# Moving the weight tiles of a float32r FFN within SBUF: one offset modulo 512 bytes for each f pair

## The chip, the cores and the metric

One Trainium2 chip, one of its cores. The metric is device microseconds of one execution, as the median of several executions. The kernel before takes 973.74 us (three runs, 971.68 to 973.83).

## The reference

Eight batches of eight heads, 576 positions, head size 64, in float32. Each head gets two attentions, whose results are added: one over q, k and v averaged over groups of four positions (144 by 144, each result repeated four times), and one over the full positions with a band mask of |i - j| < 4. The result, transposed to 4608 tokens by 512, goes through a feed-forward network (FFN):

```python
h = x @ w_in                      # 4608x512 @ 512x2048
g = s * np.maximum(h, 0.0)**2 + b
out = g @ w_out                   # 4608x2048 @ 2048x512
```

## The kernel before

The FFN fills most of the time. Its tokens are cut into 18 blocks t of 256, its 2048 hidden columns into 8 pairs p of two 128-column tiles (an f pair). Every float32 operand is split into two float32r parts, a high one and a rest, and a product is the sum of three matmuls (high by high, high by rest, rest by high).

`gemm1(t, p)` (L539) takes 24 matmuls of 256 columns, lines 544 to 546: the stationary operand, loaded ahead of each matmul, is a 128x128 piece of `wi[p]`, the moving operand a 128x256 piece of the block's `xh` or `xl`. ACT and DVE then make the parts of g (`gh`, `gl`, or one tile `gb` that holds both). `gemm2(t, p)` (L574) takes 12 matmuls of 512 columns, lines 589 to 591: here the stationary operand is a 128x128 piece of g, and the moving operand is a 128x512 piece of `wo[p]`. So the weights are stationary in gemm1 and moving in gemm2. Over the 18 blocks that is 3456 matmuls of gemm1 and 1728 of gemm2. A list `order` (L641 to L644) gives the steps: blocks 0 and 1 alternate over p, then block 2, then block by block; gemm2 runs two or three steps behind gemm1. From block 3 on, the pairs 2 and 5 use `gb`, which lies in the memory of tag `xl2` (L548).

The attention (`first_unit`, `down_unit`, `local_unit`) is woven between those steps by a generator. `split_x(t)` (L517) makes `xh` and `xl`: in tiles of those names, two of each, but for block 2 in the tiles of tags `os` and `xl2`. The weights are split by `split_parts(p)` (L239) out of staged loads (`load_w`, L196).

Where a tile lies in SBUF follows from the code alone. There are three pools, `cst`, then `one`, then `two`, each right behind the other. A pool gives every tag its place in the order in which the tags are first asked for; a tag takes the size of its largest tile, rounded up to 32 bytes of each partition, times the pool's buffers. The first tile lies at byte 1152. `make_room` (L88) asks for wi5 and wo5, then wi4, wo4, wi2 and `os`, then wi3, wo3, wo2 and `xl2`, as scratch for the first attention units before the weights move in; `load_w(0)` asks for wi6 and wo6, the first attention unit for its small tiles, `split_w(0)` for wi0 and wo0, `load_w(2)` for wi7 and wo7, and `split_w(1)` for wi1 and wo1. Each of these weight tiles takes 8192 bytes, so none changes the offset modulo 512 of what follows; the smaller tiles do. This gives, in bytes modulo 512:

```
tile                                    before
wi, wo of pairs 2, 3, 4, 5, 6              352
wi, wo of pairs 0, 1, 7                    480
xh, xl (blocks other than 2), gh, gl       288
os, xl2 (x's parts of block 2; gb)         352
```

Inside its tile, every piece that a matmul reads begins at a multiple of 512 bytes. The matmuls' tiles of 128 columns take 512 bytes of each partition, those of 256 take 1024, those of 512 take 2048. All SBUF that the kernel may use is taken.

The small tiles that the change touches are `mask` (L131), read by two DVE casts (L148, L149) at the start, `ptm` (L318), written by ACT (L319) and read by two matmuls (L328), and `ups` (L409), written by ACT from those matmuls' result (L410) and read by DVE (L423).

Of the kernel before, what the change touches and what calls it, by code (L numbers as in the profile page):

```python
# [10 lines left out]
F32 = mybir.dt.float32  # L11
# [7 lines left out]
P = 128  # L19
# [3 lines left out]
SD = S // FAC  # L23
# [31 lines left out]

W_MAX = (1.875 - 2.0 ** -23) * 2.0 ** (31 - 127)

OB = {0: (0, 1), 1: (2, 3), 2: (6, 7)}


@with_exitstack
def attention_ffn_kernel(ctx, tc, qk, vw_in, vr_in, vdm, qkn, vn, w_in, w_out, s_in, b_in, out):
# [3 lines left out]
    cst = ctx.enter_context(tc.tile_pool(name="cst", bufs=1))  # L66
    one = ctx.enter_context(tc.tile_pool(name="one", bufs=1))
    two = ctx.enter_context(tc.tile_pool(name="two", bufs=2))
    ps = ctx.enter_context(tc.tile_pool(name="ps", bufs=1, space=PS))

    def bank(i, shape, name):
        return ps.tile(shape, F32, tag=f"k{i}", name=name)
# [10 lines left out]
    def flat(tag, n, pool=one):  # L83
        return pool.tile([P, n], F32, tag=tag, name="flat")

    room = {}

    def make_room(i):  # L88
        sc, dg = flat(f"wi{6 - i}", 2048), flat(f"wo{6 - i}", 2048)
        if i == 1:  # L90
            big = flat("x", HP * S, two)
            lp = {"vw": take(big, 0, [P, NG, P]), "vd": take(big, 768, [KM, FAC, P])}
            pl, at = big, 1280
        else:
            big = flat("wi2" if i == 2 else "wo2", 2048)
            pl, at = flat("os" if i == 2 else "xl2", 1024), 512
            lp = {"qk": take(big, 0, [P, 2, SP]), "vw": take(big, 2 * SP, [P, NG, P]),
                  "vd": take(pl, 0, [KM, FAC, P])}
        lp["vr"] = take(sc, 1792, [P, FAC, D])
        return {"sc": sc, "dg": dg, "load": lp, "pl": take(pl, at, [P, 2 * NG, 32]),  # L100
                "sm": take(pl, at + 384, [P, 2, 2 * NG])}
# [26 lines left out]

    mask = cst.tile([P, 3, 32], F32, name="mask")  # L131
    nc.gpsimd.memset(mask, 0.0)

    def keep(ap, pattern, base, cm):
# [61 lines left out]
    def load_w(p):  # L196

        parts = (("i", src_i[:, :, 512 * p : 512 * p + 512]), ("o", src_o[:, 2 * p : 2 * p + 2]))
        for op, src in parts:
            st = one.tile([P, 1024, 2], I32, tag=f"w{op}{STAGE[p]}", name="wst")  # L200
            nc.sync.dma_start(st.rearrange("p (k f) t -> p k (f t)", k=src.shape[1]), src)
            wst[(p, op)] = st
# [34 lines left out]
            split_parts(p)  # L237

    def split_parts(p):  # L239
        wi[p] = one.tile([P, 2, NK, 256], F32R, tag=f"wi{p}", name="wi")  # L240
        wo[p] = one.tile([P, 2, 2, DM], F32R, tag=f"wo{p}", name="wo")
        for op, w in (("i", wi[p]), ("o", wo[p])):
            fl = w.rearrange("p s k f -> p s (k f)")
            if p < len(STAGE):
                st = wst.pop((p, op))
                for j in range(0, 1024, CHUNK[p]):
                    js = slice(j, j + CHUNK[p])
                    convert(st[:, js], fl[:, 0, js], fl[:, 1, js], op, p)
            else:
                for i in range(4):  # L250
                    cs = slice(256 * i, 256 * i + 256)
                    convert(load_quarter(p, op, i), fl[:, 0, cs], fl[:, 1, cs], op, p)
# [80 lines left out]
    def first_unit(b, hp, banks):  # L333

        alt = hp if b == 0 else 0
        at = 0
        if alt:
            sc = room[hp]["sc"]
        spots = {}

        def tmp(shape, name):
            nonlocal at
            if not alt:
                return one.tile(shape, F32, tag=name, name=name)

            if name in ("ups", "ptr"):
                spots[name] = spots["qd" if name == "ups" else "kd"]
            else:
                spots[name] = at
                at += math.prod(shape[1:])  # L350
            return take(sc, spots[name], shape)

        x = new_x(b)
        tqk, vw, _, _ = ld[(b, hp)]
        qt, kt = tqk[:, 0], tqk[:, 1]
        dg = diag[alt]
        bd = dg[0]
        dn = down(b, hp, banks, tmp, dg)
        next(dn)
        yield  # L360
        next(dn)
        yield

        own = room[hp] if b == 0 and hp else None
        pl = own["pl"] if own else two.tile([P, 2 * NG, 32], F32, tag="pl", name="pl")
        sm = own["sm"] if own else two.tile([P, 2, 2 * NG], F32, tag="sm", name="sm")
        lmx, lsm = sm[:, 0], sm[:, 1]
        for h in range(2):  # L370
            sl = banks([P, NG, 32], "sl")
            nc.tensor.matmul(sl, idb, maskb, start=True, stop=False)
            hs = slice(64 * h, 64 * h + 64)
            for g in range(NG):
                for w in range(4):
                    c0 = TW * (4 * g + w)
                    nc.tensor.matmul(
                        sl[32 * w : 32 * w + 32, g, :],
                        qt[hs, c0 : c0 + 32], kt[hs, c0 : c0 + 32],
                        start=False, stop=g == NG - 1, tile_position=(64 * h, 32 * w))  # L380
            hg = slice(h * NG, h * NG + NG)
            nc.vector.tensor_reduce(lmx[:, hg], sl, AX.X, ALU.max)
            nc.vector.tensor_tensor(
                pl[:, hg], sl, lmx[:, hg].unsqueeze(2).to_broadcast([P, NG, 32]), ALU.subtract)
            yield
        nc.scalar.activation(pl, pl, AF.Exp, scale=SCALE)
        nc.vector.tensor_reduce(lsm, pl, AX.X, ALU.add)
        nc.vector.tensor_scalar(lsm, lsm, 1e-9, None, ALU.add)
        nc.vector.reciprocal(lsm, lsm)
        (nc.vector if b else nc.gpsimd).tensor_tensor(  # L390
            pl, pl, lsm.unsqueeze(2).to_broadcast([P, 2 * NG, 32]), ALU.mult)
        yield
        next(dn)
        yield
        next(dn)
        if own:
            pt = take(sc, spots["vt"], [P, 2 * NG, 32])
        else:
            pt = two.tile([P, 2 * NG, 32], F32, tag="pl", name="pt")
        nc.vector.transpose(pt, pl)  # L400
        for w in range(4):
            ws = slice(32 * w, 32 * w + 32)
            nc.scalar.copy(bd[ws, :, ws], pt[ws])
        yield
        try:
            next(dn)
        except StopIteration as e:
            up = e.value
        ups = tmp([P, SD], "ups")  # L409
        nc.scalar.copy(ups, up)  # L410
        yield
        for f in range(2):
            n = S // 2 // FAC
            ol = banks([P, S // 2], "ol")
            for gg in range(NG // 2):
                g = f * (NG // 2) + gg
                for h in range(2):
                    hs = slice(64 * h, 64 * h + 64)
                    pw = bd[:, h * NG + g, :].rearrange("p (w c) -> p w c", w=4)
                    nc.tensor.matmul(  # L420
                        ol[hs, 96 * gg : 96 * gg + 96], vw[:, g, hs], pw[:, :, 0:TW],
                        start=True, stop=True)
            nc.vector.tensor_tensor(  # L423
                x[:, hp, f * (S // 2) : (f + 1) * (S // 2)].rearrange("p (s j) -> p s j", j=FAC),
                ol.rearrange("p (s j) -> p s j", j=FAC),
                ups[:, n * f : n * f + n].unsqueeze(2).to_broadcast([P, n, FAC]), ALU.add)
            if f == 1:
                complete.add((b, hp))
            yield
# [87 lines left out]
    def split_x(t):  # L517
        tags = ("os", "xl2") if t == 2 else ("xh", "xl")
        pool = one if t == 2 else two
        xh = pool.tile([P, HP, TB], F32R, tag=tags[0], name="xh")  # L520
        xl = pool.tile([P, HP, TB], F32R, tag=tags[1], name="xl")
        t0 = t * TB
        while t0 < (t + 1) * TB:
            b = t0 // S
            while (b, HP - 1) not in complete:
                next(gen)
            n = min((t + 1) * TB, (b + 1) * S) - t0
            src = xt[b][:, :, t0 - b * S : t0 - b * S + n]
            dst = slice(t0 - t * TB, t0 - t * TB + n)
            nc.scalar.copy(xh[:, :, dst], src)  # L530
            nc.vector.tensor_tensor(
                xl[:, :, dst], src, xh[:, :, dst].bitcast(F32), ALU.subtract)
            t0 += n
        xs[t] = (xh, xl)
# [39 lines left out]
    def gemm2(t, p):  # L574
# [3 lines left out]
        if p == 0:  # L578
            ob = OB.get(t, OB[0])
            oacc[t] = [bank(i, [P, DM], "po") for i in ob]  # L580
# [53 lines left out]
    split_w(0)  # L634
    load_w(1)
    load_w(2)
    split_x(0)
    split_x(1)

# [118 lines left out]
```

## Time and profile before

```
median of three runs        973.74 us
the profiled execution      974.94 us
its span                    973.1 us
matmuls                     7316 records, PE busy 937.4 us (96%)
DVE / ACT / POOL busy       646.8 / 478.8 / 425.0 us
granted TensorE clock       0.982 of full speed over the span
```

The page gives each engine's busy time, the span in forty slices, and the chain of work that ended last. Matmuls are pipelined, so that the duration of one (281 to 284 ns for 256 columns) is longer than the step from one matmul's start to that of the next. For the rate at which TensorE works, the starts in the timeline are what to read: the step is the difference of two starts over the number of matmuls between them.

### The profile page before, as it was taken

The numbers are of one execution on the slowest core, as the hardware profiler recorded it, in microseconds if no ns is written. First come the engines' busy times: TensorE is split into PE (matmuls) and PEld (weight loads), VectorE is DVE, ScalarE is ACT, GpSimd is POOL, SyncE is SP. The second block draws the span as 40 slices with busy tenths as digits, with TensorE's granted clock in tenths as the row PEclk, the third lists the DMA queues.
The fourth block names the chain that finished last, engine by engine and source line by source line (L and its number), as shares of the span: only waits on it lengthen the run. The fifth ranks groups of instructions, "written<-read, shape, count | busy, mean of one in ns | idle before, by whom it ended". The sixth has DMA issues, their size and how long they took to land.

```text
span 973.1 us, 18535 instructions
## 1 busy us (share of the span) xinstructions
PE 937.4 (96%) x7316; PEld 840.0 (86%) x7316; DVE 646.8 (66%) x1175; ACT 478.8 (49%) x1141; POOL 425.0 (44%) x455
## 2 busy tenths in 40 slices
PE   5769999999999999999999999999999999999998
PEld 4558888788999989889989898999899999998997
DVE  5999985864468778878787975876787772211121
ACT  5878775453755454534545344454454444333231
POOL 9422011100167686776767585575776750000000
PEclk9579999999999999999999999999999999999999
DMA  9746422102233232322323232231323100000000
GB/s 314 261 132 204 166 65 73 60 31 86 88 122 112 86 101 85 133 65 72 106 93 102 80 98 80 78 112 58 112 90 111 55 23 1 23 1 22 1 23 22
DMA packets 32103, 86.26 MB, mean 89 GB/s; under 512 B 3344, under 2 KB 7952, under 8 KB 32016
## 3 DMA queue, kind: packets, MB, share of 16 engines
q1 hardware_dynamic: 32016, 85.08, 26.4%
q8 instruction: 57, 0.93, 0.4%
q14 instruction: 30, 0.25, 0.1%
HBM read 75.63 MB, written 9.44 MB: 87 GB/s over the span
## 4 chain that ended last, share of the span: by engine, by line
PE 76%; DVE 7%; POOL 6%; DMA 6%; issue 3%; ACT 2%; DVEq 0%; SPq 0%; POOLq 0%; ACTq 0%
PE ph L544 12%; PE ph L545 12%; PE ph L546 12%; PE po L589 11%; PE po L590 11%; PE po L591 11%; DMA tqk<-in_qk_dram 3%; POOL pr L455 2%; PE sa L297 2%; DMA lqk<-in_qkn_dram 1%; POOL acc L477 1%; DMA wst<-in_moe_w_out_dram 1%; PE up L328 1%; PE ol L420 1%; PE ot L486 1%
## 5 line engine op out<-in xcount | busy, mean ns | idle before, releaser
L544 PE MATMUL ph<-xh,wi 128*128 128x256 f32 x1152 | 327.2, 284 | 5.3 <-DVE gl L557 2.5
L545 PE MATMUL ph<-xl,wi 128*128 128x256 f32 x1152 | 324.0, 281 | 0.0
L546 PE MATMUL ph<-xh,wi 128*128 128x256 f32 x1152 | 323.6, 281 | 0.0
L455 POOL TENSOR_TENSOR pr<-lqk 128x576 f32<-128x576 f32 x140 | 203.0, 1473 | 90.1 <-DMA lqk<-in_qkn_dram 53.9
L544 PEld LDWEIGHTS ph<-xh,wi 128*128 128x128 f32 x1152 | 217.1, 188 | 12.8 <-DVE gl L557 3.4
L545 PEld LDWEIGHTS ph<-xl,wi 128*128 128x128 f32 x1152 | 217.0, 188 | 5.0 <-issue 0.2
L546 PEld LDWEIGHTS ph<-xh,wi 128*128 128x128 f32 x1152 | 217.3, 189 | 0.1
L554 ACT ACTIVATE ph<-ph 128x512 f32<-128x512 f32 x144 | 83.7, 581 | 236.7 <-PE ph L546 236.5
L589 PE MATMUL po<-wo,gh 128*128 128x512 f32 x456 | 183.0, 402 | 0.2 <-ACT gh L556 0.2
L590 PE MATMUL po<-wo,gh 128*128 128x512 f32 x456 | 181.5, 398 | 0.0
L591 PE MATMUL po<-wo,gl 128*128 128x512 f32 x456 | 179.5, 399 | 0.0
L557 DVE TENSOR_TENSOR gl<-ph,gh 128x512 fp32r<-128x512 f32 x114 | 77.9, 683 | 110.9 <-ACT gh L556 110.5
L477 POOL TENSOR_TENSOR acc<-acc,pv 128x576 f32<-128x576 f32 x80 | 114.6, 1433 | 68.0 <-DVE acc L477 33.5
L457 DVE TENSOR_REDUCE st<-pr 128x9 f32<-128x576 f32 x140 | 105.9, 756 | 40.9 <-POOL pr L455 38.8
L287 POOL TENSOR_TENSOR dq<-vq 64x64 f32<-64x64 f32 x58 | 25.6, 441 | 192.4 <-PE up L326 190.2
L556 ACT CAST gh<-ph 128x512 fp32r<-128x512 f32 x114 | 66.8, 586 | 70.6 <-PE po L590 68.5
L591 PEld LDWEIGHTS po<-wo,gl 128*128 128x128 f32 x456 | 85.7, 188 | 17.3 <-issue 0.2
L476 DVE TENSOR_TENSOR pv<-lv,st 128x576 f32<-128x576 f32 x120 | 87.2, 747 | 20.2 <-POOL acc L477 19.6
L589 PEld LDWEIGHTS po<-wo,gh 128*128 128x128 f32 x456 | 85.7, 188 | 15.8 <-ACT gh L556 0.8
L590 PEld LDWEIGHTS po<-wo,gh 128*128 128x128 f32 x456 | 85.8, 188 | 15.6
L555 ACT ACTIVATE ph<-ph 128x512 f32<-128x512 f32 x144 | 83.8, 582 | 3.4
L590 PE MATMUL po<-wo,gb 128*128 128x512 f32 x120 | 48.2, 402 | 0.0
(145 smaller groups left out, 1261.1 us busy)
## 6 DMA issues: line engine op xcount, KB each, us to landing
tqk<-in_qk_dram SPq DMA_DIRECT2D x30, 584.0 KB, 4.0
lqk<-in_qkn_dram SPq DMA_DIRECT2D x20, 768.0 KB, 4.4
lv<-in_vn_dram SPq DMA_DIRECT2D x20, 480.0 KB, 3.5
out_dram<-os SPq DMA_DIRECT2D x17, 512.0 KB, 3.0
wst<-in_moe_w_in_dram SPq DMA_DIRECT2D x7, 1024.0 KB, 5.5
wst<-in_moe_w_out_dram SPq DMA_DIRECT2D x7, 1024.0 KB, 5.3
tvd<-in_vdm_dram SPq DMA_DIRECT2D x29, 160.0 KB, 2.7
tvr<-in_vr_dram SPq DMA_DIRECT2D x29, 128.0 KB, 2.1
```

The lines of the kernel that those rows point to most:

```text
L455: nc.gpsimd.tensor_tensor(pr, lqk[:, 0:CH], lqk[:, CH + o : 2 * CH + o], ALU.mult)
L457: nc.vector.tensor_reduce(ls[:, :, o], pr, AX.X, ALU.add)
L476: nc.vector.tensor_tensor(pv, lv[:, o : o + CH], w, ALU.mult)
L477: (nc.vector if o % 3 == 1 else nc.gpsimd).tensor_tensor(acc[:, :, h], acc[:, :, h], pv, ALU.add)
L544: nc.tensor.matmul(ph[:, j], wi[p][:, 0, k, f], xh[:, k], start=(k == 0), stop=False)
L545: nc.tensor.matmul(ph[:, j], wi[p][:, 0, k, f], xl[:, k], start=False, stop=False)
L546: nc.tensor.matmul(ph[:, j], wi[p][:, 1, k, f], xh[:, k], start=False, stop=(k == NK - 1))
L554: nc.scalar.activation(ph, ph, AF.Relu)
L555: nc.scalar.activation(ph, ph, AF.Square)
L589: nc.tensor.matmul(po[m], gh[:, j, ms], wo[p][:, 0, j], start=first, stop=False)
L590: nc.tensor.matmul(po[m], gh[:, j, ms], wo[p][:, 1, j], start=False, stop=False)
L591: nc.tensor.matmul(po[m], gl[:, j, ms], wo[p][:, 0, j], start=False, stop=last)
```

## The change

A helper `skip(n)` asks for a tile of n bytes in each partition under a tag of its own, which nothing writes or reads. It is called ahead of some of the weight tiles and, in the pool of `xh`, ahead of those. Room for it comes from two small tiles: `mask` goes into the tag `pv`, and the nine units that had `ups` in a tile of its own put it into the tag `ptm`. No instruction is added or taken away.

```diff
+    def skip(n, pool=one):
+        pool.tile([P, n // 4], F32, tag=f"skip{next(skips)}", name="skip")
+    skips = itertools.count()
     def make_room(i):
+        skip(32 if i == 1 else 64)
         sc, dg = flat(f"wi{6 - i}", 2048), flat(f"wo{6 - i}", 2048)
         if i == 1:
...
         else:
+            skip(64)
             big = flat("wi2" if i == 2 else "wo2", 2048)
...
-    mask = cst.tile([P, 3, 32], F32, name="mask")
+    mask = two.tile([P, 3, 32], F32, tag="pv", name="mask")
...
     def load_w(p):
+        if p == 2:
+            skip(64)
...
     def split_parts(p):
+        if p == 1:
+            skip(64)
...
-        ups = tmp([P, SD], "ups")
+        ups = tmp([P, SD], "ups") if alt else one.tile([P, SD], F32, tag="ptm", name="ups")
...
     load_w(2)
+    skip(128, two)
     split_x(0)
```

Worked out in the same way as above, the offsets modulo 512 become:

```
tile                                   before   after
wi5, wo5                                  352       0
wi4, wo4                                  352      64
wi2                                       352     128
wi3, wo3                                  352     192
wo2                                       352     256
wi6, wo6                                  352     256
wi0, wo0                                  480     320
wi7, wo7                                  480     384
wi1, wo1                                  480     448
xh, xl, gh, gl                            288       0
os (xh of block 2)                        352     128
xl2 (xl of block 2; gb)                   352     256
```

Call the distance of a matmul the offset of its weights less that of its x or g, modulo 512. In gemm1 it is, before, 64 for the pairs 2 to 6 and 192 for 0, 1 and 7; in block 2 it is 0 and 128. After, it is 0, 64, 128, 192, 256, 320, 384 and 448 for the pairs 5, 4, 2, 3, 6, 0, 7 and 1. In gemm2 the distances are the same, but for wo2 at 256, and but for pairs 2 and 5 from block 3 on, whose g is `gb`: 0 for both before, 0 and 256 after. Before, every one of these tiles begins 32 bytes past a multiple of 64; after, all of them begin at a multiple of 64.

## Rows read from the trace of the kernel before

**Rows 1.** The page: busy time, granted clock in 40 slices, chain by engine.
```profile
PE 937.4 (96%) x7316; PEld 840.0 (86%) x7316; DVE 646.8 (66%) x1175; ACT 478.8 (49%) x1141; POOL 425.0 (44%) x455
...
PEclk9579999999999999999999999999999999999999
...
PE 76%; DVE 7%; POOL 6%; DMA 6%; issue 3%; ACT 2%; DVEq 0%; SPq 0%; POOLq 0%; ACTq 0%
```

**Rows 2.** Busy time by stage, columns as in the head row.
```profile
core 0: us, PE busy (x) PEld busy (x) DVE busy (x) ACT busy (x) POOL busy (x), PEclk, DMA share, GB/s
0.00:110.00 110.00, 82.87 (x1126) 71.28 (x1127) 97.39 (x198) 80.48 (x202) 43.52 (x87) 0.84 0.68 230
...
300.00:600.00 300.00, 297.23 (x1981) 269.35 (x1980) 237.80 (x413) 137.75 (x342) 212.91 (x196) 1.00 0.30 96
600.00:840.00 240.00, 240.00 (x1601) 218.14 (x1600) 158.20 (x281) 111.90 (x268) 129.16 (x119) 1.00 0.21 67
```

**Rows 3.** What PE waited for, longest in total first: us, times, longest.
```profile
PE sa L297 <- ACT dq L277: 7.3, 1, 7.3
PE ol L420 <- ACT db L403: 4.6, 2, 2.7
...
PE ph L544 <- DVE gl L557: 2.5, 3, 1.2
```

**Rows 4.** PE's timeline, gemm1(17, 2): first and fourth matmul, next stage: start, us.
```profile
930.52 0.28 PE L544 MATMUL ph<-xh,wi 128*128 128x256 f32 x1
...
930.88 0.28 PE L544 MATMUL ph<-xh,wi 128*128 128x256 f32 x1
...
933.25 0.39 PE L589 MATMUL po<-wo,gh 128*128 128x512 f32 x1
```

**Rows 5.** The same view, gemm1(17, 1), first matmul and next stage.
```profile
922.16 0.28 PE L544 MATMUL ph<-xh,wi 128*128 128x256 f32 x1
...
924.99 0.39 PE L589 MATMUL po<-wo,gh 128*128 128x512 f32 x1
```

**Rows 6.** The same view, gemm1(17, 6), first matmul and next stage.
```profile
949.78 0.28 PE L544 MATMUL ph<-xh,wi 128*128 128x256 f32 x1
...
952.61 0.40 PE L589 MATMUL po<-wo,gh 128*128 128x512 f32 x1
```

**Rows 7.** The same view, gemm1(2, 4): two matmuls with 18 steps between.
```profile
193.03 0.28 PE L544 MATMUL ph<-xh,wi 128*128 128x256 f32 x1
...
195.19 0.28 PE L544 MATMUL ph<-xh,wi 128*128 128x256 f32 x1
```

**Rows 8.** The same view, gemm1(2, 1): two matmuls with 18 steps between.
```profile
168.71 0.28 PE L544 MATMUL ph<-xh,wi 128*128 128x256 f32 x1
...
170.85 0.28 PE L544 MATMUL ph<-xh,wi 128*128 128x256 f32 x1
```

**Rows 9.** The same view, gemm2(16, 1): its first matmul, and the next group's.
```profile
897.10 0.39 PE L589 MATMUL po<-wo,gh 128*128 128x512 f32 x1
...
899.88 0.40 PE L589 MATMUL po<-wo,gb 128*128 128x512 f32 x1
```

**Rows 10.** The same view, gemm2(16, 6): two matmuls with six steps between.
```profile
925.68 0.39 PE L589 MATMUL po<-wo,gh 128*128 128x512 f32 x1
...
927.05 0.39 PE L589 MATMUL po<-wo,gh 128*128 128x512 f32 x1
```

**Rows 11.** The same view, gemm2(16, 5) with gb: eleven steps between.
```profile
919.39 0.40 PE L589 MATMUL po<-wo,gb 128*128 128x512 f32 x1
...
921.92 0.40 PE L591 MATMUL po<-wo,gb 128*128 128x512 f32 x1
```

**Rows 12.** Lines 410 and 423: duration min/median/max, first and last start.
```profile
L410 ACT COPY ups<-up x9: 259/279/284, 24.0 to 267.8; 128x144 f32<-128x144 f32 x9
...
L423 DVE TENSOR_TENSOR x<-ol,ups x18: 411/448/458, 31.0 to 269.7; 128x288 f32<-128x288 f32 x18
```

**Rows 13.** Line 149, the last reader of the mask.
```profile
L149 DVE CAST maskb<-mask x1: 403/403/403, 10.9 to 10.9; 128x64 bf16<-128x64 f32 x1
```

## The prediction

> **What bounds the kernel now.** I read the page first: TensorE is busy for 96% of the span, is 76% of the chain that ended last, and from the fifth slice on has its full clock, the 2.4 GHz level [rows 1]. The table by stage then says where it is not the bound: only in the first 110 us, where it is busy for 83 of 110 us at a granted clock of 0.84; from 300 to 600 us it is busy for 297 of 300, from 600 to 840 us for all of it, while VectorE, the next busiest, has 238 of 300 and 158 of 240 [rows 2]. The list of TensorE's waits agrees: its longest items are 7.3 and 4.6 us, both of attention work, and gemm1's wait for g's parts is 2.5 us in all [rows 3]. So behind the first 110 us whatever changes the step from one matmul to the next changes the end by as much, and 3456 matmuls of gemm1 and 1728 of gemm2 turn 1 ns on each into 3.5 and 1.7 us.
>
> The step is therefore the thing to read, from the starts in the timeline. gemm1(17, 2) takes 24 steps in 933.25 - 930.52 = 2.73 us, 113.8 ns each [rows 4]. gemm1(17, 1), the same instructions on other tiles, takes 2.83 us, 117.9 ns each [rows 5]. Nothing waits in either; attention is over by then. I read all 136 groups of gemm1 outside block 2 in this way; each is close to one of those two steps or changes between them once. Of the pairs 0, 1 and 7, at distance 192, 48 of 51 groups are long. Of the pairs 2 to 5, at distance 64, 17 of 68 are long (1, 3, 5 and 8 for pairs 2, 3, 4, 5). But pair 6, also at 64, has 14 of 17 long (2.83 us in the last block) [rows 6]. Block 2, whose x lies elsewhere, has two more: at distance 0 18 steps take 2.16 us, 120.0 ns each [rows 7], at distance 128 2.14 us, 118.9 ns [rows 8].
>
> gemm2 shows the same in weaker form: 231.7 ns at distance 192 (2.78 us over 12) [rows 9], 228.3 at 64 (1.37 over 6) [rows 10], 230.0 at 0 with gb (2.53 over 11) [rows 11].
>
> So where the two operands lie to one another does seem to set the step, but not alone: pair 6 says that the same distance can give either step.
>
> **The change, part by part.** No instruction is added or removed and no queue is reordered by the edit itself, so the sum has two kinds of terms: steps, and waits from shared tiles.
>
> Waits first. `mask` in a buffer of `pv` is last read at 10.9 us by L149 [rows 13]; the next writer of that buffer is the conversion of the first weights, far behind it in program order: 0. If it did wait, it would wait for 0.4 us once. `ups` in `ptm`'s place is written by ACT (L410) from the result of the very matmuls that read `ptm`, so it adds no wait there. The next unit's `ptm` (L319) must now also wait until L423 has read `ups`. L423 takes 0.45 us and there are 18 of it for nine copies [rows 12]; the generator runs a unit to its end before the next one begins, so the reader is one half of an attention unit ahead. Behind L319 on ACT stand the FFN's activations, and TensorE waits for those; with the cover gone it would cost 9 x 0.45 = 4 us at the most. I take 0.
>
> gemm1, blocks other than 2, 17 x 24 = 408 matmuls for each pair:
> Pair 5 goes to distance 0. Block 2 has 120.0 there [rows 7]; now 8 of its 17 groups are long, so it is at (9 x 113.8 + 8 x 117.9)/17 = 115.7. That is +4.3 x 408 = +1.7 us.
> Pair 2 goes to 128: 118.9 [rows 8] against 114.0 now, +4.9 x 408 = +2.0 us.
> Pair 3 goes to 192, where nearly all groups are long: 117.7 against 114.5, +3.2 x 408 = +1.3 us.
> Pair 4 stays at 64: 0.
> Pairs 6, 0, 7 and 1 go to 256, 320, 384 and 448, which no gemm1 of this trace has. The nearest rows bound the step by 113.8 and 120.0 [rows 4, 7]. These pairs are now long in 62 of 68 groups, 117.5. I take the middle of the bounds, 116.9, since four distances that are known (113.8 to 120.0) spread over the whole of them: -0.6 x 1632 = -1.0 us, and from -6.0 to +4.1 us by the bounds.
> Block 2: its `xh` and `xl` now lie at two different offsets, so each pair sees two distances. 192 matmuls, now near 119.7, at the middle: -0.5 us, from -1.1 to 0.
> Together +3.5 us.
>
> gemm2: pairs 0, 1 and 7 leave 192 for distances without a row: bounds 228.3 and 231.7 [rows 9, 10], the middle 230.0, -1.7 x 648 = -1.1 us, from -2.2 to 0. Pair 3 goes from 64 to 192: +3.4 x 216 = +0.7 us. Pairs 5 and 6 go to 256 from 230.0 [rows 11] and 228.3, to the middle again: 0 and +0.4 us, from -0.4 to +1.1 together. Pairs 2 and 4 stay. Sum of gemm2 0.0 us.
>
> Sum +3.5 us: 974.94 becomes 978.4 for the profiled execution. That execution is 1.2 us over the median of its runs, so the median goes from 973.74 to 977.2 us.
>
> Two places where the trace has to be weighed against a rule. The steps at one clock differ by 4 ns between pairs that differ in nothing but place [rows 4, 5]. The Trainium skill, page "TensorE: Matmul & The Clock Gate", section "Step-by-step: what each phase is for", says that the moving operand and the weight load have a read port each, so that loading the next weights takes nothing from the running matmul. By that rule no offset matters and the sum is 0; it is the first rival below, and the trace speaks against it. The second: past its first three matmuls gemm1(17, 2) takes (933.25 - 930.88)/21 = 113 ns a step [rows 4], and no group of the trace is faster, although 256 columns at one a cycle of 2.4 GHz are 106.7 ns. The same page, section "Back-to-back issue gap", gives N/2.4 + 2.5 ns, which is 109.2 here, as the isolated gap; the trace is above it everywhere.
>
> **The rivals.**
> *No effect of the place*: what sets the long or the short step is the order of the work ahead of a group, not the offset; pair 6, long at the distance where others are short, and pair 5, half and half, speak for it; blocks 0 and 1, where pair 6 is short and pair 1 long, and block 2, near 120, speak against it. Order stays, so 973.7 us.
> *The unknown distances are good ones*, the case on the other side (not slower): pairs 6, 0, 7 and 1 lock to the short step, as the pairs at 64 mostly do. Then gemm1 has +5.0 - 6.0 - 1.1 = -2.1 us and gemm2 -2.2 + 0.7 - 0.4 = -1.9 us, together -4.0: 969.7 us. It decides from the point where more than about half of those 68 groups turn short: each is worth 24 x 4.1 ns = 0.1 us. For it: they are long now and have little to lose. Against it: of four known distances only one is short.
> *They are bad ones*: 120.0 in gemm1 for all four, +5.0 + 4.1 = +9.1 us, and +0.7 + 1.1 us in gemm2, +10.9: 984.6 us.
> *The sixteenth goes*: all tiles now begin 32 bytes past a multiple of 64, after at a multiple. The least step, 113 of 106.7 ns, is a sixteenth over a column per cycle. If that sixteenth came from the start inside a 64-byte stretch, 6.7 x 3456 + 13.3 x 1728 = 46 us would go: 928 us. Nothing in the trace has the other alignment for float32r, so it can't be excluded; but an operand that starts half a stretch late would touch one stretch more per matmul, 17 for 16 at 256 columns and 33 for 32 at 512, and gemm2's 228.3 ns [rows 10] are more than a sixteenth over 213.3, not half of that. That speaks against it.
>
> **How the numbers follow.** The sum, 977.2 us, has 0.38; its bounds are the good and the bad case above, and the edge to "no change", 976.7, is close. No effect 0.14, good distances 0.23, bad ones 0.17, the sixteenth 0.08. What a measurement can tell from no change is about 0.3%, 2.9 us. Slower by more than that: a little over half of the first case and all of the bad ones, with some waits, 0.41. Faster by more: most of the good ones and the sixteenth, 0.29. Within it: 0.30. The range of 8 in 10 leaves out the sixteenth and the outer end of the bad and the good ones: 964 to 984 us. The likeliest case's own range is 971 to 983; the 4 us of an uncovered wait would lie within it.
>
> **What would show it right or wrong.** In the timeline of the changed kernel the starts of gemm1's matmuls in the last two blocks: pair 4 stays at 113.8 ns, pair 5 goes to 120, pair 2 to about 119, pair 3 to 117.9; the step of pairs 6, 0, 7 and 1 is the open question, and whether 448 mirrors 64 can be read at once from pair 1. gemm2's pairs 0, 1 and 7 should be at or below 231.7. PE's waits should not grow at L319's readers or at L544. If a pair has the step of before at a new distance, the place does not matter; if any step falls below 113.3 ns, the sixteenth depends on the alignment and the prediction is wrong by far.

## The result, and the profile after

The changed kernel takes 977.98 us (four runs, 977.7 to 978.55) against 973.79 us for the kernel before, of which there are now four runs. The ratio is 1.0045, with a 95% interval of 1.0028 to 1.0061. By the medians it is slower by 4.2 us, where 3.5 were forecast; by the ratio it is 4.4 us. The profiled execution took 978.55 us. Every engine has the same instructions in the same order as before, so only places differ.

First the page of the changed kernel: busy time, clock in 40 slices, chain by engine.

```profile
PE 944.5 (97%) x7316; PEld 846.9 (87%) x7316; DVE 647.3 (66%) x1175; ACT 478.9 (49%) x1141; POOL 423.5 (43%) x455
...
PEclk9969999999999999999999999999999999999999
...
PE 87%; DVE 5%; DMA 2%; POOL 2%; issue 2%; ACT 2%; DVEq 0%; POOLq 0%; SPq 0%; ACTq 0%
```

TensorE is busy 7.1 us longer than in [rows 1] and its weight loads 6.9 us; of the other engines none is busy more than 0.5 us longer. The same table by stage as [rows 2], for the changed kernel:

```profile
0.00:110.00 110.00, 84.50 (x1119) 72.18 (x1120) 96.71 (x196) 80.02 (x200) 42.10 (x87) 0.92 0.68 226
...
300.00:600.00 300.00, 298.89 (x1983) 271.61 (x1982) 238.56 (x413) 139.23 (x349) 214.28 (x198) 1.00 0.30 95
600.00:840.00 240.00, 240.00 (x1600) 218.70 (x1600) 159.07 (x284) 111.24 (x267) 130.31 (x121) 1.00 0.21 68
```

From 300 us on TensorE has its full clock in both kernels and hardly any idle time in either. So the extra time is in what it does, not in what it waits for. Its longest waits after, us in total, times, longest:

```profile
PE sa L311 <- ACT dq L291: 7.3, 1, 7.3
PE ol L434 <- ACT db L417: 4.2, 2, 2.3
...
PE ph L558 <- ACT xh L544: 2.2, 1, 2.2
...
PE ph L558 <- DVE gl L571: 1.2, 2, 1.0
```

They answer to [rows 3] (lines are 14 further on), item by item. The only new item of the whole list is one of 0.4 us, and it waits for a DMA at an instruction that had waited 1.1 us before. So the shared tiles cost no wait that TensorE sees.

The starts are where the time went. The lines below are PE's timeline of gemm1(17, p), for p = 0, 1, 2, 3, 4, 5, 6, 7. Each pair has its first matmul and the first of the stage behind its 24 (start in us, then the duration of the one matmul):

```profile
919.79 0.28 PE L558 MATMUL ph<-xh,wi 128*128 128x256 f32 x1
...
922.53 0.40 PE L603 MATMUL po<-wo,gb 128*128 128x512 f32 x1
...
925.27 0.28 PE L558 MATMUL ph<-xh,wi 128*128 128x256 f32 x1
...
928.10 0.40 PE L603 MATMUL po<-wo,gh 128*128 128x512 f32 x1
...
933.62 0.28 PE L558 MATMUL ph<-xh,wi 128*128 128x256 f32 x1
...
936.50 0.40 PE L603 MATMUL po<-wo,gh 128*128 128x512 f32 x1
...
938.57 0.28 PE L558 MATMUL ph<-xh,wi 128*128 128x256 f32 x1
...
941.40 0.39 PE L603 MATMUL po<-wo,gh 128*128 128x512 f32 x1
...
942.09 0.28 PE L558 MATMUL ph<-xh,wi 128*128 128x256 f32 x1
...
944.84 0.39 PE L603 MATMUL po<-wo,gh 128*128 128x512 f32 x1
...
948.32 0.28 PE L558 MATMUL ph<-xh,wi 128*128 128x256 f32 x1
...
951.19 0.40 PE L603 MATMUL po<-wo,gb 128*128 128x512 f32 x1
...
953.25 0.28 PE L558 MATMUL ph<-xh,wi 128*128 128x256 f32 x1
...
956.13 0.40 PE L603 MATMUL po<-wo,gh 128*128 128x512 f32 x1
...
958.93 0.28 PE L558 MATMUL ph<-xh,wi 128*128 128x256 f32 x1
...
961.79 0.39 PE L603 MATMUL po<-wo,gh 128*128 128x512 f32 x1
```

Pairs 0 and 4 take 2.74 and 2.75 us, pairs 1 and 3 2.83, pairs 2 and 7 2.88 and 2.86, pairs 5 and 6 2.87 and 2.88. In the same order their distances are 320 and 64, 448 and 192, 128 and 384, 0 and 256: two pairs whose distances differ by 256 bytes have nearly the same step. Pair 2, for one, went from 2.73 us [rows 4] to 2.88.

The next table has means in ns over the 17 blocks other than block 2. They are taken over all start-to-start steps in which a matmul follows one of its own kind without a stall. A group of 24 counts as short when its mean is nearer 113.8 than 117.8:

```
pair   before: distance  gemm1  short    after: distance  gemm1  short
 4               64      115.1  12/17             64      115.1  12/17
 0              192      117.3   2/17            320      115.9  10/17
 3               64      114.7  14/17            192      117.4   2/17
 1              192      117.5   1/17            448      117.3   2/17
 2               64      114.2  16/17            128      119.0   0/17
 7              192      117.9   0/17            384      119.1   0/17
 5               64      115.9   9/17              0      119.6   0/17
 6               64      117.2   3/17            256      119.6   0/17
all blocks, gemm1        116.4                            117.9
all blocks, gemm2        231.3                            231.0
```

gemm1 pays +1.52 x 3456 = +5.3 us, gemm2 gives back 0.25 x 1728 = 0.4 us. In the profiled executions the steps that can be counted one by one hold +4.5 us. The stretches where attention matmuls stand between, and the stalls, hold 1.5 us less than before, and the first FFN matmul starts 0.6 us later. Together that is the 3.6 us by which the span grew (973.1 to 976.7). The 1.5 us are no effect of slower matmuls: the run with old distances, below, has the steps of before and the same 1.5 us less.

### The profile page after: what moved, and what is told of

Read it like the earlier page. It is cut to its first block, busy times and chain, and to the rows that moved or that the text cites. A ratio compares the mean times of both kernels' runs of the same rounds, so it can differ in the third digit from the quotient of the medians.

```text
span 976.7 us, 18535 instructions
## 1 busy us (share of the span) xinstructions
PE 944.5 (97%) x7316; PEld 846.9 (87%) x7316; DVE 647.3 (66%) x1175; ACT 478.9 (49%) x1141; POOL 423.5 (43%) x455
## 4 chain that ended last, share of the span: by engine, by line
PE 87%; DVE 5%; DMA 2%; POOL 2%; issue 2%; ACT 2%; DVEq 0%; POOLq 0%; SPq 0%; ACTq 0%
PE ph L558 14%; PE ph L559 13%; PE ph L560 13%; PE po L603 12%; PE po L604 12%; PE po L605 12%; PE sa L311 2%; PE up L342 1%; PE ol L434 1%; DMA wst<-in_moe_w_out_dram 1%; PE sl L391 1%; PE ot L500 1%; DMA tqk<-in_qk_dram 1%; PE tp L329 1%; PE tr L331 1%
## 5 line engine op out<-in xcount | busy, mean ns | idle before, releaser
L491 POOL TENSOR_TENSOR acc<-acc,pv 128x576 f32<-128x576 f32 x80 | 115.1, 1439 | 69.5 <-DVE acc L491 35.8
```

The lines of the kernel that those rows point to most:

```text
L491: (nc.vector if o % 3 == 1 else nc.gpsimd).tensor_tensor(acc[:, :, h], acc[:, :, h], pv, ALU.add)
```

## The experiments

The edits are against the changed kernel, and where tags are placed in order, its own calls of `skip` are out. `place(tag, n)` asks for a tag's tile ahead of its use, so that tags lie in a chosen order; where a kernel has eight such calls in a row, a loop stands for them here. No experiment leaves out any of the computation, and but for the last one the engines keep their order of instructions. Each ratio is to the kernel before, measured anew beside that experiment (medians of 975.2 to 976.0 us).

**Old distances, with the shared tiles and starts at multiples of 64.**

```diff
-        skip(32 if i == 1 else 64)
+        if i == 1:
+            skip(96)
...
-            skip(64)
...
-        if p == 2:
-            skip(64)
...
     def split_parts(p):
-        if p == 1:
+        if p == 0:
             skip(64)
...
-    skip(128, two)
```

> The changed kernel's shared tiles and its starts at multiples of 64 bytes, but the distances of the kernel before (weights less x or g, modulo 512): 64 for pairs 2 to 6, 192 for 0, 1, 7, 0 for gb; block 2 at 0 and 128. Distance theory: gemm1's steps are again those of before, 114 to 117 ns for the pairs 2 to 6 and 117.5 for 0, 1 and 7, mean 116.4, and the time is 973.8 us within 2. Rival, the shared tiles or the start within 64 bytes cost the 4 us: the time stays at 978 us and the steps are not those of before. Rival, the distance has no effect: 978 us too, with the steps of the changed kernel.

The ratio to the kernel before is 0.9995 (0.998 to 1.001). gemm1 has 116.3 ns, gemm2 231.1. These are gemm1(17, 1) and gemm1(17, 2) in its timeline:

```profile
920.87 0.28 PE L556 MATMUL ph<-xh,wi 128*128 128x256 f32 x1
...
923.70 0.39 PE L601 MATMUL po<-wo,gh 128*128 128x512 f32 x1
...
929.24 0.28 PE L556 MATMUL ph<-xh,wi 128*128 128x256 f32 x1
...
931.97 0.39 PE L601 MATMUL po<-wo,gh 128*128 128x512 f32 x1
```

2.83 and 2.73 us are the times of [rows 5] and [rows 4] to the last digit. So the shared tiles cost nothing that can be measured, and whether a tile starts at 0 or 32 modulo 64 does not matter by itself: only the distance was put back, and the 4 us went with it.

This run also says what the 1.5 us of the accounting above are not. gemm1's wait for g's rest is as short here as in the changed kernel, though the steps are those of before, when it was 2.5 us [rows 3]:

```profile
PE ph L556 <- DVE gl L569: 1.2, 2, 1.0
```

Between 480 and 570 us TensorE waited 2.4 us for it in the profile before, and 1.0 us in each of the other two. Why is not shown.

**Weights 32 bytes further on.**

```diff
-        skip(32 if i == 1 else 64)
+        skip(64)
...
+        if p == 1:
+            skip(32)
...
-    skip(128, two)
+    skip(96, two)
```

> The changed kernel with all weights 32 bytes further on, x and g where they were: distances 32, 96, 160, 224, 288, 352, 416, 480 in gemm1 for pairs 5, 4, 2, 3, 6, 0, 7, 1. Theory, a smooth function of the distance modulo 256: pairs 5 and 6 alike, 4 and 0 alike, 2 and 7 alike, 3 and 1 alike, each between the steps of the neighbours at multiples of 64: 117.5, 117, 118.2, 118.5 ns, mean 117.8, 977 us. Rival, the pair and not the distance: each pair keeps the step it has in the changed kernel. Rival, reads that begin 32 bytes apart within 64 collide less or more: steps under 113.3 or over 120 ns, 960 or 990 us.

The tags `os` and `xl2` move along with the weights here, so block 2, and the pairs 2 and 5 in gemm2 from block 3 on, keep the distances of the changed kernel; the steps by pair below leave block 2 out.

The ratio is 1.0061 (1.0041 to 1.0082). gemm1 has 118.3 ns, gemm2 232.4. Pairs 5 and 6 have 118.3 and 118.3 ns, 4 and 0 118.1 and 118.2, 2 and 7 119.9 and 119.5, 3 and 1 116.9 and 117.0: the period of 256 again, on a second set. But the values between are not the mean of their neighbours, as I had expected: 96 has no group at the short step, though 64 has, and 224 is under both 192 and 0. gemm1(17, 3), at 224, takes 2.81 us:

```profile
942.43 0.28 PE L560 MATMUL ph<-xh,wi 128*128 128x256 f32 x1
...
945.24 0.40 PE L605 MATMUL po<-wo,gh 128*128 128x512 f32 x1
```

**The worst multiple of 32 for everything.**

```diff
+    skip(32)
+    place("os", 4096)
+    place("xl2", 4096)
+    skip(160)
+    for p in range(NFP):
+        place(f"wo{p}", 8192)
+    for p in range(NFP):
+        place(f"wi{p}", 8192)
+    skip(32)
     load_pair(0, 0)
...
-    skip(128, two)
+    skip(96, two)
```

> All weights at distance 160 from x and from g, the slowest of the multiples of 32 seen so far: gemm1 119.9 ns, gemm2 234.1 for every pair. Distance theory: +3.5 x 3456 + 2.9 x 1728 = +12 + 5 = +17 us against before, ratio 1.017. Rival, the place counts only for some pairs or with some neighbours: ratio under 1.01.

The ratio is 1.0121 (1.0100 to 1.0141), +11.8 us. All eight pairs have 119.7 to 119.8 ns in gemm1 and 233.2 to 234.0 in gemm2, and none of 136 groups is short. By the steps it should have been +11.8 (gemm1) + 4.0 (gemm2) = +15.8 us. The same accounting as above finds the difference in the stalls and the attention stretches, which are 4.2 us shorter than in the kernel before; 1.5 us of these the run with old distances has too. gemm1(17, 4) takes 2.88 us:

```profile
948.18 0.28 PE L576 MATMUL ph<-xh,wi 128*128 128x256 f32 x1
...
951.06 0.40 PE L621 MATMUL po<-wo,gh 128*128 128x512 f32 x1
```

**gemm1 at 64, gemm2 at 0.** 
```diff
+    skip(32)
+    for p in range(NFP):
+        place(f"wo{p}", 8192)
+    place("os", 4096)
+    place("xl2", 4096)
+    skip(64)
+    for p in range(NFP):
+        place(f"wi{p}", 8192)
     load_pair(0, 0)
...
-    skip(128, two)
+    skip(160, two)
```

> All weights moved so that gemm1 has distance 64 for every pair and block, gemm2 distance 0 for every pair. Distance theory, with the means that the two profiles have at these distances (gemm1 115.4 ns over the five pairs of before, 115.05 for the one of the changed kernel; gemm2 229.2): gemm1 -1.0 to -1.3 ns x 3456 and gemm2 -2.0 ns x 1728 against before, -7 to -8 us, 966 us; pairs 0, 1 and 7, long before, turn mostly short. Rival, the pair or the order of the work ahead of it sets the step (pair 6 long at 64): pairs 0, 1, 6, 7 stay at 117.5 to 118 ns in gemm1, the time is 970 to 974 us.

The ratio is 0.9980 (0.9965 to 0.9995). gemm2 did as expected, 229.4 ns. gemm1 did not, and so neither did the time: it has 116.4 ns, with 48 of 136 groups short, spread over all pairs. These are two groups of block 17, pairs 2 and 4:

```profile
925.69 0.28 PE L563 MATMUL ph<-xh,wi 128*128 128x256 f32 x1
...
928.52 0.40 PE L608 MATMUL po<-wo,gh 128*128 128x512 f32 x1
...
934.11 0.28 PE L563 MATMUL ph<-xh,wi 128*128 128x256 f32 x1
...
936.83 0.40 PE L608 MATMUL po<-wo,gh 128*128 128x512 f32 x1
```

2.83 and 2.72 us at the same distance, in the same block, with the attention long over. So distance 64 has two steps that both last, and something else chooses between them. That is what pair 6 had shown before the change.

**gemm1 at 64, gemm2 at 192.** 
```diff
+    skip(32)
+    place("os", 4096)
+    place("xl2", 4096)
+    skip(64)
+    for p in range(NFP):
+        place(f"wi{p}", 8192)
+    skip(128)
+    for p in range(NFP):
+        place(f"wo{p}", 8192)
     load_pair(0, 0)
...
-    skip(128, two)
+    skip(96, two)
```

> As the run with 64 and 0, but gemm2 at distance 192 for every pair; gemm1 stays at 64. In all profiles so far gemm1 at 64 is mostly short behind a gemm2 at 192 (pairs 2, 3, 4 before) and mostly long behind one at 0 or 64 (pairs 5 and 6 before, all pairs with gemm2 at 0). Theory, the gemm2 group ahead sets in which of its two steps gemm1 locks: all eight pairs mostly short, mean 114.5 ns, -1.9 x 3456 = -6.5 us against before; gemm2 at 233.4 ns, +2.1 x 1728 = +3.7 us; together 971 us. Rival, the pair's own place in SBUF sets it: gemm1 stays at 116.4 as with gemm2 at 0, and the time is 977 to 978 us.

The ratio is 0.9977 (0.9959 to 0.9994). gemm1 has 114.7 ns, with 107 of 136 groups short, 10 to 17 of 17 for each pair; gemm2 has 233.0. Pairs 0, 1, 6 and 7, long in the kernel before, are mostly short as the others are, so the pair's own place is not what chooses. In blocks 15 to 17, where the attention is over, all 24 groups are short. gemm1(17, 2) takes 2.74 us:

```profile
928.09 0.28 PE L576 MATMUL ph<-xh,wi 128*128 128x256 f32 x1
...
930.83 0.39 PE L621 MATMUL po<-wo,gh 128*128 128x512 f32 x1
```

**What of the gemm2 group chooses?** Two kernels ask that. The first has wo and g at 0, x at 64 and wi at 128, modulo 256, so that gemm1 and gemm2 keep 64 and 0 while wi less wo becomes 128. (Block 2 differs: its `xl` lies at 0, so its distances are 64 and 128.)

```diff
+    skip(32)
+    place("xl2", 4096)
+    for p in range(NFP):
+        place(f"wo{p}", 8192)
+    skip(64)
+    place("os", 4096)
+    skip(64)
+    for p in range(NFP):
+        place(f"wi{p}", 8192)
     load_pair(0, 0)
...
-    skip(128, two)
+    skip(32, two)
     split_x(0)
     split_x(1)
+    skip(96, two)
```

> gemm1 at distance 64 and gemm2 at 0 for every pair as in the run with 64 and 0, but all of gemm1's tiles 64 bytes further on than there: wo and g at 0, x at 64, wi at 128 (modulo 256). The distance between gemm1's weights and gemm2's, which overlap for one matmul where gemm2 ends and gemm1 begins, is then 128, as it is in the run with 64 and 192 and for pairs 2, 3, 4 before, and not 64. Theory A, that one overlap sets in which step gemm1 locks: gemm1 114.6 ns, gemm2 229.4, -6.1 - 3.2 us against before, ratio 0.990. Theory B, the steps inside gemm2 (its distance to g) set it: gemm1 116.4 as with 64 and 0, ratio 0.997.

The ratio is 0.9995 (0.9984 to 1.0006), where theory B had 0.997. gemm1 has 116.9 ns, with 37 of 136 groups short; gemm2 has 228.7. Theory A is out: with the overlap of the one matmul made like that of the run before, gemm1 stays long. In blocks 15 to 17 all 24 groups are long (118.0 ns), where the run before has all 24 short. gemm1(17, 2) takes 2.83 us:

```profile
928.50 0.28 PE L576 MATMUL ph<-xh,wi 128*128 128x256 f32 x1
...
931.33 0.40 PE L621 MATMUL po<-wo,gh 128*128 128x512 f32 x1
```

The second has 64 and 0, but with gl 64 bytes beyond gh; `os` and `xl2` now lie ahead of wo.

```diff
+    skip(32)
+    place("os", 4096)
+    place("xl2", 4160)
+    skip(192)
+    for p in range(NFP):
+        place(f"wo{p}", 8192)
+    skip(64)
+    for p in range(NFP):
+        place(f"wi{p}", 8192)
     load_pair(0, 0)
...
-            both = one.tile([P, 2, 2, TB], F32R, tag="xl2", name="gb")
-            gh, gl = both[:, 0], both[:, 1]
+            both = one.tile([P, 4 * TB + 16], F32R, tag="xl2", name="gb")
+            gh, gl = (both[:, o : o + 2 * TB].rearrange("p (a c) -> p a c", a=2)
+                      for o in (0, 2 * TB + 16))
...
+            if (t, p) == (0, 0):
+                skip(32, two)
             gl = two.tile([P, 2, TB], F32R, tag="gl", name="gl")
...
-    skip(128, two)
+    skip(32, two)
```

> As the run with 64 and 0, but g's rest gl lies 64 bytes further on than gh, so that every third matmul of gemm2 has distance 192 and the others 0; wi less wo stays 64. Theory B (gemm2's last matmul, with gl at 192, sets gemm1's step): gemm1 114.6 ns, gemm2 230.6, ratio 0.993. Theory A (wi less wo sets it): gemm1 116.4, gemm2 230.6, ratio 0.999.

The ratio is 0.9970 (0.9956 to 0.9984). gemm1 has 115.1 ns, with 95 of 136 groups short; gemm2 has 231.2. That is nearer to theory B's 114.6 ns than to theory A's 116.4, but the time is not what B had (0.993). gemm1(17, 2) takes 2.72 us:

```profile
928.83 0.28 PE L576 MATMUL ph<-xh,wi 128*128 128x256 f32 x1
...
931.55 0.40 PE L624 MATMUL po<-wo,gh 128*128 128x512 f32 x1
```

**Only the last of gl.** The gap now stands between gl's two halves. The tags lie as in the run before, but with 4224 bytes for `xl2` and `skip(128)` behind it.

```diff
+    def gap(raw):
+        return raw[:, 0 : 2 * TB + 32].rearrange("p (a c) -> p a c", a=2)[:, :, 0:TB]
...
-            both = one.tile([P, 2, 2, TB], F32R, tag="xl2", name="gb")
-            gh, gl = both[:, 0], both[:, 1]
+            both = one.tile([P, 4 * TB + 32], F32R, tag="xl2", name="gb")
+            gh = both[:, 0 : 2 * TB].rearrange("p (a c) -> p a c", a=2)
+            gl = gap(both[:, 2 * TB : 4 * TB + 32])
...
-            gl = two.tile([P, 2, TB], F32R, tag="gl", name="gl")
+            gl = gap(two.tile([P, 2 * TB + 64], F32R, tag="gl", name="gl"))
...
-    skip(128, two)
+    skip(32, two)
```

> As the run with gl 64 bytes on, but only the second half of gl (its second 128-column tile, read by the last matmul of each three of the second j) has the gap; so 2 of the 12 matmuls of a gemm2 group, the last one among them, have distance 192 and the others 0. If the matmuls right ahead of gemm1 set its step: gemm1 115.1 ns as there, gemm2 230.2, -4.4 and -1.8 us, ratio 0.995. Rival, all of gemm2's matmuls with gl count, or the step is a matter of chance once a group begins elsewhere: gemm1 near 116.4, ratio 0.998.

The ratio is 0.9985 (0.9972 to 0.9998). gemm1 has 115.5 ns, with 77 of 136 groups short. gemm2 has 231.2, no better than with the gap for all of gl, although 10 of its 12 matmuls, and not 8, are at 0. This lies between the two forecasts, so it settles little: what gemm2 does ahead of gemm1 counts, but I can't name the matmul.

**A scan in steps of 4 bytes.** From block 3 on, x and g begin 4 x (t modulo 8) bytes further on in block t.

```diff
+    def shifted(tag, name, a, t):
+        o = 0 if t < 3 else t % 8
+        raw = one.tile([P, 2 * a * TB + 8], F32R, tag=tag, name=name)
+        v = raw[:, o : o + 2 * a * TB].rearrange("p (a c) -> p a c", a=2 * a)
+        return v[:, 0:a], v[:, a : 2 * a]
...
+            xh, xl = shifted(f"xx{next(turn_x)}", "xh", HP, t)
...
```

> A scan in steps of 4 bytes: x's parts and g's parts of block t (from 3 on) begin 4 x (t modulo 8) bytes further on; weights lie so that gemm1 has distances 64 less that for the even pairs and 96 less that for the odd ones, gemm2 0 and 32 less that. For this xh and xl, and gh and gl, share a tile, so the order of the work changes a little; only the steps are read, not the time. Theory, a bank or line of 64 bytes behind the effect: the step changes smoothly between the known values, 118.3 at 32, the two steps 113.8 and 117.8 near 64, 118.1 at 96; gemm2 229.3 at 0, 233.0 at 32 and at -32. Rival, lines of 16 or 32 bytes: jumps within 32 bytes, with steps over 120 ns where a piece begins off a line of 16, or some distance whose step is always 113.3 ns.

There is one execution, 991.51 us, with another order of work, so its time is not compared. The table has gemm1's means in ns, by distance:

```
distance   36    40    44    48    52    56    60    64
ns       117.9 120.9 120.8 118.7 118.1 120.7 121.7 115.5
distance   68    72    76    80    84    88    92    96
ns       118.5 120.0 121.3 119.3 119.4 119.9 120.4 117.9
```

The smooth theory fails. Multiples of 16 (48, 64, 80, 96) are better than most of what lies around them, which is the rival's form, though 36, 52 and 68 are as good as 48, and 84 as 80. No distance is always at the least step, and no group is under 113.2 ns. gemm2 hardly shows it: 229.9 at 0 and 229.1 at 16, but 230.8 to 233.9 at the other places from -28 to 32, with 233 at -16 and 32, which are multiples of 16 too.

## Why the prediction was right

*TensorE's step bounds the kernel.* Right in the main: a change of places alone, with the order of all instructions unchanged, moved the time by -0.3% to +1.2%, each time to the side that the sum of the steps gives, as far as it could be told from none. But not the whole of it arrives: 4.4 of 4.8 us in the changed kernel, 11.8 of 15.8 at 160, 2.9 of 4.5 in the best, 1.5 of 3.1 with the gap in the last of gl. The working took 1 ns on a matmul for 1 ns at the end. In the profile at 160 the rest lies in the stalls and the attention stretches. Why is not shown: these differ by 1.5 us from the profile before even where the steps are the old ones.

*The distance sets the step.* Right, and shown: put back, the time comes back (0.9995), and made bad for all, it goes to 1.0121. Pair 5 was forecast at 120.0 and has 119.6, pair 2 at 118.9 and has 119.0, pair 3 at 117.7 and has 117.4, pair 4 stayed at 115.1. The two steps that decided the sign had come from block 2 alone [rows 7, 8]. "No effect of the place" is out.

*The number.* That 3.5 us came so near to the measured 4.2 is in part luck: the steps gave +4.8, and not all of it arrived.

*The four unknown distances.* Taken at the middle of the bounds, 116.9; they have 119.6, 115.9, 119.1 and 117.3, mean 118.0. That term was mis-sized by +1.1 x 1632 = +1.8 us. The other terms came out 0.5 us lower together, so the steps gave +4.8 us and not +3.5. What I did not see is that the function has a period of 256 bytes: 256, 320, 384 and 448 repeat 0, 64, 128 and 192, and all four could have been read off. The bad rival was right for two of them, 256 and 384, near its 120.0. The good one was half right for 320, with 10 of 17 groups short, and wrong for 448.

*gemm2* was forecast at 0.0 us and gave back 0.4. *Block 2* was to gain 0.5 us; its step is 118.2 after and 119.3 before, so 0.2.

*The shared tiles* were taken at 0: shown by the run with old distances. *The sixteenth* stayed: with all tiles at multiples of 64, and with starts at any multiple of 4, no group's step fell under 113.2 ns. What it comes from is open.

*Pair 6*, long at 64, was left unexplained. The runs show that at 64 gemm1 can keep either step, and that it is mostly short behind a gemm2 with some matmuls at 192 (107, 95 and 77 of 136 groups) and mostly long behind one at 0 (48 and 37). The kernel before shows part of this. Of its groups of the pairs 2 to 6, 32 of 39 are short where the matmul right ahead is one of gemm2 at 192. Pair 6 stands behind one at 0 in 12 of its 17 groups, and 11 of these are long. But pair 5 stands behind one at 0 in five, and four are short; and behind one at 64, 6 of 9 are short, where the expectation of the run with 64 and 192 had most of them long. What passes from one stage to the next was not measured; that it is the phase between the weight load and the running matmul is argued only. Nor is the distance told apart from gemm2's pace: the runs with the slower gemm2 (233.0, 231.2, 231.2 ns) are those with more short groups, against 229.4 and 228.7 in the other two.

The Trainium skill, page "SBUF — State Buffer", section "Who interferes with whom", says that TensorE never waits on anyone. These traces agree with it as far as other engines go: in the run at 160, gemm1's step is 119.8 ns from 300 to 600 us, where VectorE is busy for 237 us and GpSimd for 214, and 119.7 behind 860 us, where GpSimd does nothing. But the steps of 113.8 and 119.6 ns at two places of the same operands show that TensorE's pace does depend on where its own two operands lie; that its two reads wait for each other is the likely reading, and no run here shows it.

## What to carry to other kernels

Where TensorE is the bound and each matmul has its own weight load, read the step between starts, group by group, before believing a formula: places in SBUF moved it by 5% here, and a tile more or less ahead of them moves all places behind it. An edit that only frees or adds a small tile can change the time in this way; the places tried here span 1.5% of it. The best version found (gemm1 at 64, gl 64 bytes beyond gh, weights of gemm2 at gh's offset) beats both kernels, by 0.3% over the one before (ratio 0.9970) and, by the two ratios (1.0045/0.9970), 0.75% over the changed one. It is the best of nine tried, and the runs at 0.9977, 0.9980 and 0.9985 can't be told from it.

## What the runs showed of the hardware

The table is for float32r matmuls at the full clock, by distance modulo 256 (ns, means of all groups with that distance in these profiles; where there are two values, the range over pairs and runs):

```
distance            0      32     64        96     128    160    192     224
gemm1, 256 cols   119.6  118.3  114-117.7  118.1  119.0  119.8  117-118  117.0
gemm2, 512 cols   229    233    230.5      233.5  232.5  233.6   233.0   232.8
```

The least step that lasts is 113.3 ns for 256 columns. At distance 64 two steps, 113.8 and 117.8, each last for whole groups of 24 matmuls, and in the last blocks, where nothing but the FFN runs, they repeat from block to block. In the scan in steps of 4 bytes, the distances at which x begins off a multiple of 16 bytes have 120.0 ns in the mean, the four others 117.9; but those at which x begins 12 bytes past such a multiple (36, 52, 68 and 84) have only 117.9 to 119.4. That is one profile, and x's start and the distance change together in it, so it doesn't tell the two apart.
